# An MLP kernel whose first eight rows open with two token tiles, the third tile's input being loaded later

## The chip, the cores and the metric

The kernel runs on one core of one Trainium2 chip. The metric is the device time of one execution, in microseconds (us); the median of three runs before the change is 396.4 us (396.39, 396.40 and 397.09).

## What is computed

A channel MLP on 2048 tokens of 1024 channels, with a hidden width of 3584, all in bf16:

```python
def reference(x, w1, b1, w2, b2):
    y = _layernorm(x, axis=-1)            # over the 1024 channels, eps 1e-5
    h = _gelu(jnp.einsum("bsd,df->bsf", y, w1) + b1)     # tanh form
    return jnp.einsum("bsf,fd->bsd", h, w2) + b2
```

x is (1, 2048, 1024), w1 (1024, 3584), w2 (3584, 1024).

## The kernel before

Tokens are taken in 16 tiles of 128, four tiles to a block of 512 columns. The 1024 channels are eight groups of 128, called dt 0 to 7 here. The hidden units are 28 rows of 128. The first product of a block is made row by row: a row is eight matmuls, one for each dt, that accumulate in one PSUM bank (`pe_row`, L382). Gelu on ScalarE (`act_gelu`, L407) empties the bank to `hT_sb`, and the second product (`out_chunk`, L449) follows. Every engine has a program written out by hand in `_Prog` lists; for VectorE alone, the part after the first block's opening is merged from two lists (`crit` and `fill`) by estimated times.

The first eight rows of block 0 are made in another way, called the wave, because the input must first be loaded, transposed and normalised:

- Tiles 0, 1 and 2 are the raw tiles. TensorE transposes them as they were loaded (`pe_T`, L336), ScalarE copies the transposes from PSUM to `yT_sb` (L352), and the wave's matmuls (`pe_wave`, L397) run on values that aren't normalised. A cell is one row and one dt. Two columns of ones stand ahead of tile 0, so a cell on tiles 0 to 2 is 386 columns wide, a cell on tiles 0 and 1 is 258, and one on tile 2 alone is 128.
- Mean and variance of the raw tiles are taken on VectorE (`op_stats` L248, `op_aggr` L258), the power for the reciprocal deviation on GpSimd (L255). `ops_row_turn` (L480) turns them into rows, and `put_row_spread` (L486, ScalarE) spreads the rows over the partitions. `ops_fix` (L536 and L539) then corrects each wave row in PSUM, first by the mean and then by the deviation.
- Tile 3 is normalised before its matmul. VectorE does its statistics, its normalisation (L262) and a 32 by 32 block transpose (L490); ScalarE, VectorE and GpSimd move the blocks to their places (`put_moves_3` L507, `moves_3` L498 and L495). Its 64 cells of 128 columns come last in the wave, row by row, followed by each row's fix and gelu.
- From row 8 on, block 0 uses centred copies of the raw tiles, made by `ops_centre` (L529) on VectorE: four pieces, ctr0 to ctr3, of two dt each.

VectorE's order in the opening is one list:

```python
seq = st[0] + st[1] + st[2] + turn_m[:2] + st[3] + turn_m[2:] + nm[3] + moves_3() + turn_r + ctr[:2]
```

then the fixes of rows 0 and 1, ctr2 and ctr3, and the fixes of rows 2 to 7.

All loads but b1's are issued by SP on one queue, in the order of `SP_FIRST_LOADS`; x0 to x3 are 256 KB, and w0 to w8 are the nine pieces of w1 that the wave needs: w0 and w1 (128 KB each) hold dt 0 and dt 1 for rows 0 to 3, w2, w3 and w4 (256 KB) hold dt 2 and 3, 4 and 5, 6 and 7 for the same rows, and w5 to w8 hold the same for rows 4 to 7. The eight rows have the eight PSUM banks; from row 8 on, six banks are used in a ring, so row 8 waits for the gelu of row 0, and row 13 for that of row 7.

TensorE's order in the opening is: 25 matmuls on constants (L471), a small transpose for b1, the transposes of tiles 0, 1 and 2, four cells (rows 0 to 3 at dt 0) on tiles 0 and 1 and the same four on tile 2, then 28 cells of 386 columns (rows 0 to 3, dt 1 to 7), 32 of 386 columns (rows 4 to 7), and the 64 cells of tile 3.

Of the kernel before, what the change touches and what calls it, by code (L numbers as in the profile page):

```python
# [9 lines left out]
I32 = mybir.dt.int32  # L10

LN_EPS = 1e-5
P = 128
# [6 lines left out]
TAIL_PIECES = (448, 64)  # L20
RAW = (0, 1, 2)
N_WARM = 25
GROUPS_0 = (0, 4, 8)
GROUPS_2 = (0, 2, 8)
HALVES = (0, 4, 8)
PIECES = ((0, 1, (0, 1, 2, 3)), (1, 2, (0, 1, 2, 3)), (2, 4, (0, 1, 2, 3)), (4, 6, (0, 1, 2, 3)), (6, 8, (0, 1, 2, 3)),
          (0, 2, (4, 5, 6, 7)), (2, 4, (4, 5, 6, 7)), (4, 6, (4, 5, 6, 7)), (6, 8, (4, 5, 6, 7)))
CENTRE = (0, 2, 4, 6, 8)
DVE_MOVES = ((0, 0), (1, 1), (2, 2))
POOL_MOVES = ((3, 3), (0, 1), (1, 2), (2, 3))  # L30
W1_COLS = (512, 1024, 1024)
N_W2_CHUNKS = 4
SP_FIRST_LOADS = ("b1", "x0", "x1", "x2", "w0", "w1", "w2", "w3", "x3", "w4", "w5", "w6", "w7", "w8")
N_ONES = 2
PAD = 64

# [56 lines left out]
def bass_standalone__mixer_channel_mlp__prompt_kernel(  # L93
# [13 lines left out]
    DT = D // P  # L107
# [7 lines left out]
    R = R_WAVE  # L115
    assert R == NB1 + NB2 + 1 and R < FT
    assert NB1 + NB2 + 1 <= 8 and NB2 == 2
    assert all(c[-1] == DT for c in (GROUPS_0, GROUPS_2, HALVES))
    assert TPB == 4 and RAW == (0, 1, 2)

    w1_chunks = [(j0, j1, rows[0] * P, (rows[-1] + 1) * P) for j0, j1, rows in PIECES]
# [21 lines left out]
    with ExitStack() as es:  # L143
# [6 lines left out]
        yT_sb = sb("yT_sb", [P, 2, DT, PAD + TB], BF16)  # L150
# [26 lines left out]
        act = _Prog("s_act")  # L177
# [34 lines left out]
        def issue(item):  # L212
            if item == "b1":
                dma_q[0] = act
                dma(b1r_sb[:, :], b1.rearrange("(t p) -> t p", p=P), "b1", F * 2)
                dma_q[0] = sp
            elif item[0] == "x":
                load_x_tile(int(item[1:]))
            elif item[0] == "w" and int(item[1:]) < len(w1_chunks):
                load_w1(int(item[1:]))  # L220

        act.op(lambda e: e.preload_act_table(ACT.Gelu_apprx_tanh))
        for item in SP_FIRST_LOADS:
            issue(item)
# [8 lines left out]
        for b in range(2, NB):  # L233
# [4 lines left out]
                sig="ident")  # L238
# [53 lines left out]
        ybuf = lambda b: (b + 1) % 2  # L292
# [16 lines left out]
        def dve_put(o):  # L309
# [3 lines left out]
        bank_read = {}  # L313
        bank_of = {"t": ps_t[:, 0, :], "2_0": ps_2b[:, 0, :], "2_1": ps_2b[:, 1, :], "1_1": ps_1b[:, 1, :], "1_2": ps_1b[:, 2, :], "1_3": ps_1b[:, 3, :],
                   "1_4": ps_1b[:, 4, :]}
        ycol = lambda i: PAD + (i % TPB) * P
# [3 lines left out]
        def pe_T(i, groups, banks):  # L320
            blk = i // TPB
            src_ev = y_ev[i] if i in y_ev else [x_ev[i][0]] * DT
            evs = yT_ev.setdefault(i, [None] * DT)
            prev = None
            for k, (g0, g1) in enumerate(zip(groups[:-1], groups[1:])):
                bname = banks[k]
                for j in range(g0, g1):
                    waits = []
                    if bname != prev:
                        waits = ["ident"] + ([bank_read[bname]] if bname in bank_read else [])  # L330
                        off = 0
                    prev = bname
                    if j == g0 or src_ev[j] != src_ev[j - 1]:
                        waits.append(src_ev[j])
                    last = j == g1 - 1 and (k + 1 == len(banks) or banks[k + 1] != bname)
                    pe.op(lambda e, i=i, j=j, o=off, bap=bank_of[bname]: e.transpose(  # L336
                        out=bap[:, o:o + P], in_=x_sb[:, i, j * P:(j + 1) * P], identity=ident[:, :]),
                        waits=waits, sig=(f"tp{i}_{k}" if last else None))
                    evs[j] = f"te{i}_{k}"
                    off += P  # L340
            off = 0
            prev = None
            for k, (g0, g1) in enumerate(zip(groups[:-1], groups[1:])):
                bname = banks[k]
                if bname != prev:
                    off = 0
                prev = bname
                done = max(m for m in range(len(banks)) if banks[m] == bname)
                src = bank_of[bname][:, off:off + (g1 - g0) * P].bitcast(I32)
                src = src.rearrange("p (j s) -> p j s", j=g1 - g0)  # L350
                dst = yT_sb[:, 0 if i in RAW else ybuf(blk), g0:g1, ycol(i):ycol(i) + P].bitcast(I32)
                act.op(lambda e, dst=dst, src=src: e.copy(out=dst, in_=src), waits=[f"tp{i}_{done}"],  # L352
                       sig=f"te{i}_{k}")
                off += (g1 - g0) * P
                bank_read[bname] = f"te{i}_{k}"
            pe_t[0] += DT * 0.056

        unit_n = [0]
        bank_gelu = {}
# [4 lines left out]
        def new_unit():  # L364
            u = unit_n[0]
            unit_n[0] += 1
            bank = first_ring[u] if u < len(first_ring) else ring[(u - len(first_ring)) % len(ring)]
            waits = [bank_gelu[bank]] if bank in bank_gelu else []
            name = "t" if bank[0] == "t" else f"{bank[0]}_{bank[1]}"
            if not waits and name in bank_read:  # L370
                waits.append(bank_read[name])
            return bank, waits
# [16 lines left out]
        def pe_wave(r, dt, tiles, bank, waits, sig):  # L389
            raw = tiles[0] == 0  # L390
            base = raw_at if tiles[0] in RAW else 0
            y0 = ycol(tiles[0]) - (N_ONES if raw else 0)
            n0 = base + y0 - ycol(RAW[0]) if tiles[0] in RAW else 0
            n1 = n0 + ycol(tiles[-1]) + P - y0
            w = list(waits) + (["onecols"] if raw else []) + [yT_ev[t][dt] for t in tiles]
            w.append(f"w1c{w1_chunk_of(r, dt)}")
            pe.op(lambda e: e.matmul(  # L397
                unit_bank(bank)[:, n0:n1], lhsT=w1_sb[:, dt, r * P:(r + 1) * P], rhs=yT_sb[:, 0 if tiles[0] in RAW else ybuf(0), dt, y0:y0 + n1 - n0],
                start=(dt == 0 and tiles[0] in (0, 3)), stop=(dt == DT - 1), skip_group_check=True),
                waits=w, sig=sig)  # L400
            pe_t[0] += _mm_us(n1 - n0)
            if sig:
                est[sig] = pe_t[0]
# [80 lines left out]
        def put_row_spread(k, q0, q1):  # L484
            for q in range(q0, q1):
                act.op(lambda e, q=q: e.copy(out=row_b(k)[32 * q:32 * (q + 1)], in_=row_b(k)[0:32]),  # L486
                       waits=[f"row_q{k}"], sig=(f"row_{k}" if q == 3 else None))
# [27 lines left out]
        def put_b1():  # L515
            act.op(lambda e: e.copy(out=b1_sb[:, :], in_=bank_of["1_1"][:, 0:FT]), waits=["b1t"], sig="b1c")
            bank_read["1_1"] = "b1c"
# [5 lines left out]
        def ops_centre():  # L523
            res = []
            for k, (j0, j1) in enumerate(zip(CENTRE[:-1], CENTRE[1:])):
                xt, ct = [yT_sb[:, k, j0:j1, ycol(RAW[0]):ycol(RAW[0]) + len(RAW) * P].rearrange(
# [22 lines left out]

        pe_b1()  # L550
        put_b1()
        pe_T(0, GROUPS_0, ("t", "2_0"))
        pe_T(1, GROUPS_0, ("2_1", "1_4"))
        pe_T(2, GROUPS_2, ("t", "2_0"))
        put_row_spread(0, 1, 4)
        wave = [new_unit() for _ in range(R)]
        opened = set()

        def wave_cell(r, dt, tiles, sig=None):
            waits = [] if r in opened else wave[r][1]  # L560
            opened.add(r)
            pe_wave(r, dt, tiles, wave[r][0], waits, sig)

        first = [(r, dt) for r in PIECES[0][2] for dt in range(*PIECES[0][:2])]
        for tiles in (RAW[:2], RAW[2:]):
            for r, dt in first:
                wave_cell(r, dt, tiles)
        cells = [(r, dt) for j0, j1, rows in PIECES[1:] for r in rows if r < R for dt in range(j0, j1)]
        for n, (r, dt) in enumerate(cells):
            wave_cell(r, dt, RAW, f"raw_{r}" if dt == DT - 1 else None)  # L570
        cs_ev = {}
# [26 lines left out]
        for t in RAW:  # L598
            yT_ev[t] = [f"ctr{k}" for k, (j0, j1) in enumerate(zip(CENTRE[:-1], CENTRE[1:])) for _ in range(j0, j1)]

# [5 lines left out]
        for b in range(NB):  # L606
            if b + 1 < NB:
                tiles = list(range((b + 1) * TPB, (b + 2) * TPB))
# [9 lines left out]
            for st in range(TPB):  # L618
                for dh in range(DH):
                    c0, c1 = dh * NCH, (dh + 1) * NCH  # L620
                    ob = (b * TPB + st) % NOB
                    prev = store_last.get((ob, dh))
# [14 lines left out]
        while ci < len(crit) or fi < len(fill):  # L637
            take_crit = fi >= len(fill)
            if not take_crit and ci < len(crit):
                rel_f, _, blk_f = fill[fi]  # L640
                if crit[ci][0] <= max(t_dve, rel_f) + CRIT_SLACK and blk_f > crit[ci][2]:
                    take_crit = True
            if take_crit:
                rdy, o, _ = crit[ci]
                ci += 1
            else:
                rdy, o, _ = fill[fi]
# [46 lines left out]
```

## Time and profile before

| | us |
|---|---|
| median of three runs | 396.4 |
| the profiled execution, its own time | 396.67 |
| span of its profile | 395.4 |
| TensorE busy in the span | 390.9 |
| VectorE busy | 162.0 |
| ScalarE busy | 86.2 |
| GpSimd busy | 11.7 |

The profile is of one execution. Its span is 1.27 us shorter than that execution's time. A line of the timeline gives the start, the length, the engine, the line of the kernel, the operation, what it writes and reads, and how many instructions were merged; in brackets is the idle time of the engine before it, with what ended it. A matmul's listed length includes its way through the array, so neighbours overlap, and the pitch of a series is had from a window's length by the number of matmuls in it. The view of the DMA queues gives for each issue its size and the time from issue to landing.

### The profile page before, as it was taken

To read this page: it belongs to the slowest core of one execution; us is meant where nothing else is said; L and a number is where in the kernel's file an instruction comes from. 1 tells how busy PE (TensorE), PEld (TensorE's weight loads), DVE (VectorE), ACT (ScalarE), POOL (GpSimd) and SP (SyncE) were. 2 spreads that over 40 slices of the span, in tenths; PEclk is the share of its full clock that TensorE was granted. 3 is DMA by queue.
4 is the path that set the end of the run, shared out by engine and by line. 5 is a ranking of instruction groups with operands and counts; after the bars stand their busy time and mean duration, and the time that the engine had idled before them with its cause. 6 is when DMAs were issued, how large, how long until landed. Compare 5 with 4: busy or idle time off the path is not lost.

```text
span 395.4 us, 4518 instructions
## 1 busy us (share of the span) xinstructions
PE 390.9 (99%) x1904; PEld 184.9 (47%) x1938; DVE 162.0 (41%) x338; ACT 86.2 (22%) x139; POOL 11.7 (3%) x59
## 2 busy tenths in 40 slices
PE   9999999999999999999999999999999999999998
PEld 7744444444444444444444444444444444444444
DVE  5998889988999306987100000001100000001011
ACT  3655420000144332000023443100003334400000
POOL 3101000011001100000000000000000000000000
DMA  7999940000000000000000000000000000000000
GB/s 257 373 385 386 387 155 26 16 27 14 28 0 0 2 0 0 28 26 15 28 13 2 0 0 2 13 13 28 25 15 15 0 0 2 0 15 27 13 28 27
DMA packets 16078, 23.63 MB, mean 60 GB/s; under 512 B 1082, under 2 KB 8250, under 8 KB 16058
## 3 DMA queue, kind: packets, MB, share of 16 engines
q1 hardware_dynamic: 16016, 23.33, 16.7%
q8 instruction: 15, 0.25, 0.3%
q14 instruction: 5, 0.04, 0.0%
q10 hardware_dynamic: 42, 0.01, 0.0%
HBM read 19.14 MB, written 4.19 MB: 59 GB/s over the span
## 4 chain that ended last, share of the span: by engine, by line
PE 99%; issue 0%; DVE 0%
PE ps L449 49%; PE ps L382 38%; PE ps_t L382 7%; PE ps L397 3%; PE ps L471 1%; PE ps_t L397 0%; PE ps L336 0%; PE ps_t L336 0%; DVE o_sb L460 0%; PE ps L512 0%
## 5 line engine op out<-in xcount | busy, mean ns | idle before, releaser
L449 PE MATMUL ps<-w_sb,hT_sb 128*128 128x512 bf16 (+2 forms) x909 | 193.3, 373 | 0.8
L382 PE MATMUL ps<-yT_sb,w_sb 128*128 128x512 bf16 x678 | 152.4, 379 | 0.9
L449 PEld LDWEIGHTS ps<-w_sb,hT_sb 128*128 128x128 bf16 x924 | 88.6, 98 | 105.2
L407 ACT ACTIVATE hT_sb<-ps,b_sb 128x512 bf16<-128x512 f32 x94 | 64.0, 687 | 234.4 <-PE ps L382 217.2
L382 PEld LDWEIGHTS ps<-yT_sb,w_sb 128*128 128x128 bf16 x696 | 68.0, 98 | 81.9
L460 DVE TENSOR_TENSOR o_sb<-ps,b_sb 128x512 bf16<-128x512 f32 (+2 forms) x33 | 22.3, 675 | 198.7 <-PE ps L449 198.5
L304 DVE STREAM_TRANSPOSE yT_sb<-x_sb 32x256 bf16<-32x256 bf16 x192 | 83.7, 436 | 21.9 <-PE ps_t L382 18.8
L382 PE MATMUL ps_t<-yT_sb,w_sb 128*128 128x512 bf16 x135 | 31.9, 379 | 0.1
L248 DVE BATCH_NORM_STATS2 st_sb<-x_sb 128x6 f32<-128x512 bf16 x32 | 21.0, 672 | 4.7 <-DMA x_sb<-in_x_dram 4.6
L382 PEld LDWEIGHTS ps_t<-yT_sb,w_sb 128*128 128x128 bf16 x136 | 13.3, 98 | 16.1
L407 ACT ACTIVATE hT_sb<-ps_t,b_sb 128x512 bf16<-128x512 f32 x18 | 12.4, 687 | 17.5 <-PE ps_t L382 14.6
L397 PE MATMUL ps<-yT_sb,w_sb 128*128 128x128 bf16 (+2 forms) x116 | 13.1, 269 | 0.0
L397 PEld LDWEIGHTS ps<-yT_sb,w_sb 128*128 128x128 bf16 x116 | 8.9, 98 | 3.5
L255 POOL TENSOR_TENSOR rstd_sb<-mv_sb,nhalf 128x1 f32<-128x1 f32 x13 | 7.1, 548 | 113.6 <-DVE mv_sb L258 113.6
L423 DVE TENSOR_TENSOR ps<-ps,row_r 128x384 f32<-128x384 f32 x17 | 9.2, 561 | 2.7 <-PE ps L382 2.5
L262 DVE TENSOR_SCALAR x_sb<-x_sb,mv_sb,rstd_sb 128x1024 bf16<-128x1024 bf16 x13 | 7.0, 541 | 2.0 <-POOL rstd_sb L255 1.3
L536 DVE SCALAR_TENSOR_TENSOR ps<-row_r,ncs,ps 128x384 f32<-128x384 f32 x7 | 4.2, 614 | 0.6 <-PE ps L397 0.6
L486 ACT COPY row_r<-row_r 32x384 f32<-32x384 f32 x6 | 3.1, 510 | 4.3 <-DVE row_r L480 4.2
L539 DVE TENSOR_TENSOR ps<-ps,row_r 128x384 f32<-128x384 f32 x7 | 3.9, 563 | 0.2
L529 DVE TENSOR_TENSOR yT_sb<-yT_sb,row_r 128x768 bf16<-128x768 bf16 x4 | 3.6, 950 | 0.0
L471 PE MATMUL ps<-const-bfloat16-1.0 128*128 128x128 bf16 x25 | 2.8, 309 | 0.8 <-PEq L679 0.8
L258 DVE BATCH_NORM_AGGREGATE mv_sb<-st_sb 128x2 f32<-128x15 f32 x13 | 2.9, 222 | 0.4
(34 smaller groups left out, 32.9 us busy)
## 6 DMA issues: line engine op xcount, KB each, us to landing
w_sb<-in_w_dram SPq DMA_DIRECT2D x4, 1792.0 KB, 18.3
w_sb<-in_w_dram SPq DMA_DIRECT2D x2, 2048.0 KB, 16.4
out_dram<-o_sb SPq DMA_DIRECT2D x31, 128.0 KB, 1.7
x_sb<-in_x_dram SPq DMA_DIRECT2D x3, 1024.0 KB, 14.4
w_sb<-in_w_dram SPq DMA_DIRECT2D x7, 256.0 KB, 5.4
x_sb<-in_x_dram SPq DMA_DIRECT2D x4, 256.0 KB, 3.4
w_sb<-in_w_dram SPq DMA_DIRECT2D x1, 1024.0 KB, 10.1
w_sb<-in_w_dram SPq DMA_DIRECT2D x2, 128.0 KB, 3.7
```

Of the source, the lines that this page charges most:

```text
L248: return (lambda e, i=i, h=h, pw=pw: e.bn_stats(st_sb[i][:, 6 * h:6 * (h + 1)], x_sb[:, i, h * pw:(h + 1) * pw]), [x_ev[i][h if len(x_ev[i ...
L255: pool.op(lambda e, i=i, dst=dst, mv=mv: e.tensor_tensor(out=dst, in0=mv[:, 1:2], in1=nhalf[:, i:i + 1], op=ALU.pow), waits=[f"mv{i}", "nh ...
L262: return (lambda e, i=i, c0=c0, c1=c1: e.tensor_scalar(out=x_sb[:, i, c0:c1], in0=x_sb[:, i, c0:c1], scalar1=mv_sb[:, i, 0:1], scalar2=rst ...
L304: res.append((lambda e, src=src, dst=dst: e.transpose(out=dst, in_=src), waits, (f"tr{i}" if lastop else None), 0.47))
L382: pe.op(lambda e, b=b, r=r, dt=dt, bank=bank: e.matmul(unit_bank(bank)[:, 0:TB], lhsT=w1_sb[:, dt, r * P:(r + 1) * P], rhs=yT_sb[:, ybuf(b ...
L397: pe.op(lambda e: e.matmul(unit_bank(bank)[:, n0:n1], lhsT=w1_sb[:, dt, r * P:(r + 1) * P], rhs=yT_sb[:, 0 if tiles[0] in RAW else ybuf(0) ...
L407: act.op(lambda e, r=r, n0=n0, n1=n1, bank=bank: e.activation(out=hT_sb[:, r, n0:n1], in_=unit_bank(bank)[:, n0:n1], func=ACT.Gelu_apprx_tanh,
L423: crit.append((est[sig], (lambda e, reg=reg: e.tensor_tensor(out=reg, in0=reg, in1=row_b(1), op=ALU.mult), [sig, "row_1"], ready, 0.57), 0))
L449: pe.op(lambda e, sl=sl, ft=ft, c0=c0, c1=c1, bank=bank: e.matmul(ps_2[:, bank, 0:c1 - c0], lhsT=hT_sb[:, ft, sl * P:(sl + 1) * P], rhs=w2 ...
L460: crit.append((est[sig], (lambda e, ob=ob, c0=c0, c1=c1, bank=bank: e.tensor_tensor(out=o_sb[:, ob, c0:c1], in0=ps_2[:, bank, 0:c1 - c0], ...
L471: pe.op(lambda e: e.matmul(ps_1[:, 0, 0:P], lhsT=ones, rhs=ones, start=True, stop=True))
L536: return [(lambda e: e.scalar_tensor_tensor(out=reg, in0=row_b(0), scalar=ncs[:, c:c + 1], in1=reg, op0=ALU.mult, op1=ALU.add), [f"m1_0_{r ...
```

## The change

x2 is loaded four places later and x3 one place later: the order becomes x0, x1, w0, w1, w2, w3, x2, w4, x3, w5 and so on. Tiles 0 and 1 are copied in groups of two and six dt (before: four and four), and their copies alternate between the tiles. TensorE transposes tiles 0 and 1 only, then runs 24 cells of 258 columns (dt 0 to 5 of rows 0 to 3), then the transposes of tile 2, then 8 cells of 258 columns (dt 6 and 7), then 32 cells of 128 columns on tile 2 (dt 0 and 1 of the four rows first, as these are its first group), and after that rows 4 to 7 on all three tiles, now dt by dt where they were row by row within a piece. The mean's row spread on ScalarE stands behind tile 2's copies, as before. VectorE's list for the opening is the same; in the merged part behind it some statistics of block 1 stand one place earlier or later among the multiplications of rows 13 and on.

```diff
-GROUPS_0 = (0, 4, 8)
-GROUPS_2 = (0, 2, 8)
+GROUPS = (0, 2, 8)
...
+N_EARLY = 4
+N_PAIR = 5
...
-SP_FIRST_LOADS = ("b1", "x0", "x1", "x2", "w0", "w1", "w2", "w3", "x3", "w4", "w5", "w6", "w7", "w8")
+SP_FIRST_LOADS = ("b1", "x0", "x1", "w0", "w1", "w2", "w3", "x2", "w4", "x3", "w5", "w6", "w7", "w8")
...
+        def put_copy(i, groups, banks, k):
+            g0, g1 = groups[k:k + 2]
+            bname = banks[k]
+            assert banks.count(bname) == 1
+            src = bank_of[bname][:, 0:(g1 - g0) * P].bitcast(I32)
+            src = src.rearrange("p (j s) -> p j s", j=g1 - g0)
+            dst = yT_sb[:, 0, g0:g1, ycol(i):ycol(i) + P].bitcast(I32)
+            act.op(lambda e, dst=dst, src=src: e.copy(out=dst, in_=src), waits=[f"tp{i}_{k}"], sig=f"te{i}_{k}")
+            bank_read[bname] = f"te{i}_{k}"
...
-        pe_T(0, GROUPS_0, ("t", "2_0"))
-        pe_T(1, GROUPS_0, ("2_1", "1_4"))
-        pe_T(2, GROUPS_2, ("t", "2_0"))
-        put_row_spread(0, 1, 4)
+        T_BANKS = (("t", "2_0"), ("2_1", "1_4"), ("t", "2_0"))
+        for t in RAW[:2]:
+            pe_T(t, GROUPS, T_BANKS[t])
+        for k in range(2):
+            for t in RAW[:2]:
+                put_copy(t, GROUPS, T_BANKS[t], k)
...
-        first = [(r, dt) for r in PIECES[0][2] for dt in range(*PIECES[0][:2])]
-        for tiles in (RAW[:2], RAW[2:]):
-            for r, dt in first:
-                wave_cell(r, dt, tiles)
-        cells = [(r, dt) for j0, j1, rows in PIECES[1:] for r in rows if r < R for dt in range(j0, j1)]
+        cells_of = lambda a, b: [(r, dt) for j0, j1, rows in PIECES[a:b] for dt in range(j0, j1) for r in rows]
+        for r, dt in cells_of(0, N_EARLY):
+            wave_cell(r, dt, RAW[:2])
+        pe_T(2, GROUPS, T_BANKS[2])
+        for k in range(2):
+            put_copy(2, GROUPS, T_BANKS[2], k)
+        put_row_spread(0, 1, 4)
+        for r, dt in cells_of(N_EARLY, N_PAIR):
+            wave_cell(r, dt, RAW[:2])
+        for r, dt in sorted(cells_of(0, N_PAIR), key=lambda c: (c[1] >= GROUPS[1], c)):
+            wave_cell(r, dt, RAW[2:], f"raw_{r}" if dt == DT - 1 else None)
+        cells = cells_of(N_PAIR, len(PIECES))
```

`pe_T` itself loses its copies, which `put_copy` now issues.

More of the change, by code (lines that the diff above doesn't have):

```diff
@@ L117, in bass_standalone__mixer_channel_mlp__prompt_kernel @@
     assert NB1 + NB2 + 1 <= 8 and NB2 == 2
-    assert all(c[-1] == DT for c in (GROUPS_0, GROUPS_2, HALVES))
+    assert all(c[-1] == DT for c in (GROUPS, HALVES))
     assert TPB == 4 and RAW == (0, 1, 2)
@@ L340, in pe_T @@
                     off += P
[L341 to L355, printed above, removed]
-            pe_t[0] += DT * 0.056
+            pe_t[0] += DT * 0.056
+        def put_copy(i, groups, banks, k):
[7 more added lines that the diff above has]
+            bank_read[bname] = f"te{i}_{k}"
         unit_n = [0]
```

## The prediction

> **What bounds the kernel now.** First the page's first part and its chain of waits, for the whole span:
>
> ```profile
> PE 390.9 (99%) x1904; PEld 184.9 (47%) x1938; DVE 162.0 (41%) x338; ACT 86.2 (22%) x139; POOL 11.7 (3%) x59
> ...
> PE 99%; issue 0%; DVE 0%
> ```
>
> TensorE is the bound from end to end, so an edit of the opening can win only what TensorE loses there, and can lose what it is made to wait. So I read the chain's pieces in the opening (start, length, what):
>
> ```profile
> 0.83 2.82 PE ps L471 x25
> ...
> 4.32 1.28 PE ps L336 x12
> 5.60 0.10 issue
> 5.71 0.37 PE ps_t L336 x2
> 6.08 0.47 PE ps L336 x6
> 6.54 6.22 PE ps L397 x42
> ```
>
> The reader is to see that hardly a hole is left. The last transpose of tile 1 starts at 5.29 and those of tile 2 at 5.71, when x2 has landed (5.57); at a pitch of 0.107 us that is a pause of some 0.3 us. The second loss is speed: the 16 transposes from 3.71 start 0.107 us apart, and from 6.2 us on the same form starts 0.056 apart. The granted clock reads 1.00 throughout, so I take this from the spacing. What is left of the opening is full-speed work: windows over the wave give 4.57 us for 28 cells of 386 columns (0.163 each), 0.44 for 4 cells of 258 (0.110), and 3.57 for tile 3's 64 cells of 128 (0.056).
>
> Then the timeline, for the engines that walk close beside TensorE:
>
> ```profile
> 6.40 1.22 DVE L248 BATCH_NORM_STATS2 st_sb<-x_sb 128x6 f32<-128x512 bf16 x2
> ...
> 9.07 1.28 DVE L248 BATCH_NORM_STATS2 st_sb<-x_sb 128x6 f32<-128x512 bf16 x2 [0.61 <-DMA x_sb<-in_x_dram]
> ...
> 13.14 2.75 ACT L507 COPY yT_sb<-xq_sb 32x128 int32<-32x128 int32 x9 [0.16 <-DVE xq_sb L490]
> ...
> 16.84 3.29 PE L397 MATMUL ps<-yT_sb,w_sb 128*128 128x128 bf16 x56
> ...
> 17.49 1.15 DVE L536 SCALAR_TENSOR_TENSOR ps<-row_r,ncs,ps 128x384 f32<-128x384 f32 x2 [0.58 <-PE ps L397]
> ...
> 19.48 1.81 DVE L529 TENSOR_TENSOR yT_sb<-yT_sb,row_r 128x768 bf16<-128x768 bf16 x2
> ```
>
> VectorE takes tile 2's statistics at 6.40, straight behind tile 1's, and waits only for x3 (0.61 us). From 9.07 to 16.91 it runs without a hole, ScalarE's nine moves of tile 3 hang on it and end at 15.90, and TensorE starts tile 3's cells at 16.84: 0.94 us of air. VectorE waits 0.58 us for TensorE at 17.49, and is then full until 28 us. Behind that the air is thin: ctr3 is done at 21.30 and row 8's weight load for dt 6 stands at 21.50 (0.20); the gelu of row 7 signals at 28.76 and row 13, which takes its bank, loads weights at 28.84 (0.08). A weight load takes 0.098 us and stands 0.21 ahead of its matmul, which gives some 0.1 more.
>
> Last the queue. These are x2 (issued 1.69), w3 (3.59) and x3 (4.10), with the time to landing:
>
> ```profile
> x_sb<-in_x_dram SPq DMA_DIRECT2D x1, 256.0 KB, 3.9
> ...
> w_sb<-in_w_dram SPq DMA_DIRECT2D x1, 256.0 KB, 4.3
> ...
> x_sb<-in_x_dram SPq DMA_DIRECT2D x1, 256.0 KB, 4.9
> ```
>
> In order, the last parts land at 3.52 (x0), 4.15 (x1), 5.57 (x2), 5.94 (w0), 6.29 (w1), 6.98 (w2), 7.88 (w3), 9.05 (x3), 9.79 (w4). SP issues one about every 0.5 us, 3 to 5 us ahead of landing, so the bytes ahead decide, not the issue.
>
> **The change, part by part.**
>
> *The loads.* By bytes ahead, the new order lands w0 and w1 where x2 landed (w1 by 5.57; w0 midway from 4.15, 4.9), w2 at 6.29, w3 at 6.98, x2 (sixth 256 KB) where w3 landed, 7.88, w4 at 9.05, x3 at 9.79. But x2 and x3 took 1.42 and 1.17 us behind the piece before them, w3 only 0.90; x2 at 1.42 behind 6.98 would be 8.40. I take 8.1 for x2. Its upper bound is 9.05, where the eighth load landed before; its lower, w2's 6.98 plus w2's own step, 0.69, is 7.67. The loads behind x3 keep their bytes ahead, so their landings stay.
>
> *Transposes and copies.* Tiles 0 and 1 are transposed as before, the last starting at 5.29. ScalarE copies 128x128 in 0.27 us and 128x384 in 0.48 (rows of L352), with about 0.04 between. A transpose group signals 0.33 after its last start: tile 1's first group at 4.98, its copy done at 5.28; the big copies done at 5.80 and, after a signal at 5.62, at 6.33. Before, the first cells waited for tile 1's last copy, and it cost nothing as tile 2 was being transposed; now the first cells need only 5.28 and w0 (4.9), and start at about 5.4. The pause of 0.3 us is gone.
>
> *The first 24 cells.* 258 columns at half speed take 0.107 x 258/128 = 0.215 (an estimate; no row has this form so early). Four reach 6.28. Full speed from 6.2 us as before: dt 1 to 6.72 (w1 5.57), dt 2 and 3 to 7.60 (copies 6.33, w2 6.29), dt 4 and 5 to 8.47 (w3 6.98).
>
> *Tile 2.* Its transposes start at 8.47, with x2 at 8.1 no wait, and take 8 x 0.056 to 8.92. Then the cells of dt 6 and 7 need w4, 9.05: a wait of 0.15. 8 x 0.110 brings 9.98; ScalarE's copies of tile 2 (0.27 + 0.48 behind 8.9) lie beside them. 32 x 0.056 ends at 11.76. Before, this point was 11.62. So the gain of the early start, 0.3 us of pause at half speed (0.15) and eight transposes at full instead of half speed, is spent on running four wide cells at half speed, on the w4 wait, and on 28 splits at 0.110 + 0.056 - 0.163, 0.003 each, 0.08 together. TensorE on its own: +0.14. Bounds: without the w4 wait 0.0; with x2 at 9.05, +0.6.
>
> *Rows 4 to 7 dt by dt* cost nothing: the same cells, on weights landed (w5 at 10.52 against 11.76). Only raw_4 signals later (16.5), and ScalarE asks for it after 16.9. *The merge* moves a 0.68 us statistic ahead of row 13's multiplication; that bank is next wanted at row 19, five rows of 1.73 us later. Nothing.
>
> *What is late next.* Tile 2's statistics stand ahead of x3's in VectorE's list, so x2's landing now moves all behind it. Before, from 6.40 to the end of the first two turns took 2.07 us; with x2 at 8.1 they end at 10.2, after x3 (9.79), and x3's statistics start at 10.19, not 9.07: a shift of s = 1.12 us. Bounds of s: 0.74 (x3 alone decides) and 2.07 (x2 at 9.05). The tile 3 moves end at 15.90 + 1.12 = 17.02 against TensorE's 16.98: no more than 0.05. VectorE had 0.58 us of idle before the fixes; the rest, 0.54, is a late VectorE from there, with no hole until row 7's gelu. TensorE meets it at ctr3 and at row 13, whose air is 0.08 + 0.1. So TensorE's delay is s - 0.58 - 0.18 = **s - 0.76 = 0.36 us**, the 0.14 above lying within it. After row 13 the air is over 1 us (row 14's bank frees 29.34, wanted 30.78), and what TensorE has lost stays lost.
>
> *The sum.* 396.67 + 0.36 for the profiled execution. That stands 0.27 over the median, so the forecast for the median is 396.4 + 0.36, rounded **396.75 us**.
>
> **A rule against the change.** The half-speed row first: starts of 0.107 us from 0.83 to 6.19. The Trainium skill, page "TensorE: Matmul & The Clock Gate", section "What's actually happening", says that the clock is granted by a window of about 3.4 us that runs freely, and by how busy the array was in it. The trace agrees that a pause of 0.3 us at 5.4 did not put it off. By this rule the early cells get no sooner to full speed than the transposes did, which is what the sum has.
>
> **Rivals.** (1) *The gain stays.* If x2 lands by 7.74, x3 decides, s is 0.74 and VectorE's lateness is covered; w4 then tends to be early too, and TensorE runs from 11.6: 396.4. For it: the fastest of the engines' parts of x3 was there at 7.49, so the bytes allow it. Against: the last part decides, and both x2 and x3 trailed.
>
> (2) *Slower: x2 holds VectorE.* The place is tile 2's statistics, the price s - 0.76 with s = x2 - 6.98; over 0.8 us from x2 at 8.54 on. At the bound 9.05 it is +1.31, 397.7. For it: x2 lands amid the time (7 to 9 us) in which the eighth load trailed by 1.17. Against: 256 KB less lie ahead of it.
>
> (3) *The clock falls back.* Should the changed gap at 5.4 us begin the half-speed stretch (5.4 us, 0.83 to 6.2) anew, work until 10.8 is at half speed: 4.6/2 = +2.3, 398.7. Against: the pause in the trace of before did nothing of the kind. By the Trainium skill's window of 3.4 us it would be 1.7 (an estimate).
>
> (4) *Faster beyond measure.* The opening lost 0.15 by the pause and no more than 0.8/2 = 0.4 if full speed came at 5.4; both together are 0.55, and VectorE's chain would have to come along. Only the spread of runs, 0.7 us, could show it.
>
> **How the numbers follow.** A measurement of this kernel can tell about 0.2%, 0.8 us, from no change. Forecast (x2 from 7.75 to 8.54, 396.4 to 397.2): 0.47. Rival 1: 0.16. Rival 2: 0.27. Rival 3: 0.05. Rival 4: 0.05. Within 0.2% are the forecast and rival 1, 0.63; slower 0.32; faster 0.05. The range reaches to 397.7, rival 2's bound, and to 396.1, rival 1 less the spread seen below a median; about 0.15 stays outside.
>
> **What would show it.** In the profile after: no pause of TensorE at 5.4 to 5.7; an idle VectorE from 6.5 until x2 lands, about 1.6 us, under tile 2's statistics; x3's statistics at 10.2; the fixes at 18.0, no longer waiting for TensorE; small issue gaps of TensorE at row 8's dt 6 or at row 13; row 8 of block 0 at 20.5 to 20.8, where it stood at 20.36. Everything behind 31 us is the same, shifted. Wrong it would be if x2 lands after 8.54 or before 7.7, if w0 is not there at 5.4, or if TensorE's first cells keep the 0.215 pitch beyond 6.3 us.

## The result, and the profile after

The changed kernel takes 397.5 us (median of 17 runs, 396.75 to 398.86) against 396.52 us before (17 runs, 395.98 to 397.09): a ratio of 1.0025, with a 95% interval of 1.0016 to 1.0034. That is 0.98 us slower, where the forecast had 0.36. The median is inside the stated range because the range reached to the second rival's bound, 397.7; it lies 0.75 over the forecast's 396.75. The spread of the runs has doubled, from 1.1 to 2.1 us, and the fastest changed run, 396.75, lies within the runs of before.

The profiled execution took 398.02 us, with a span of 396.8, 1.4 more than before. The first part of its page and the shares of its chain of waits:

```profile
PE 391.3 (99%) x1932; PEld 186.3 (47%) x1966; DVE 161.4 (41%) x338; ACT 86.1 (22%) x139; POOL 11.7 (3%) x59
...
PE 97%; DMA 1%; issue 1%; SPq 0%; DVE 0%
```

TensorE is busy 0.4 us longer in a span 1.4 us longer, so 1.0 us is waiting. The chain now begins in the load queue. Its pieces in the opening (start, length, what):

```profile
2.64 5.05 DMA w_sb<-in_w_dram
7.69 0.14 issue
7.83 1.92 PE ps L393 x16
...
17.93 0.16 PE ps_t L393
18.09 0.12 issue
18.21 3.29 PE ps L393 x56
```

The first line is w2, issued at 2.64 and landed at 7.69; the forecast had 6.29. The timeline of the same kernel shows what stood still (start, length, engine, line, operation; in brackets the idle time before it and what ended it):

```profile
7.83 1.92 PE L393 MATMUL ps<-yT_sb,w_sb 128*128 128x258 bf16 x16 [0.90 <-DMA w_sb<-in_w_dram]
9.12 1.29 DVE L249 BATCH_NORM_STATS2 st_sb<-x_sb 128x6 f32<-128x512 bf16 x2 [2.68 <-DMA x_sb<-in_x_dram]
...
11.26 1.29 DVE L249 BATCH_NORM_STATS2 st_sb<-x_sb 128x6 f32<-128x512 bf16 x2
...
18.18 3.14 PEld L393 LDWEIGHTS ps<-yT_sb,w_sb 128*128 128x128 bf16 x56 [0.48 <-ACT yT_sb L503]
```

TensorE waits 0.90 us for w2. VectorE waits 2.68 us for x2, which landed at 9.10 (forecast 8.1), and takes x3's statistics at 11.26 where it took them at 9.07 before: s is 2.19 us. Tile 3's cells then wait for ScalarE's moves, which hang on VectorE. They start at 18.21 against 16.84, 1.37 us late, and the rest of the kernel is shifted by as much (row 8's second cell at 21.99 against 20.63).

Both late loads stand behind a dip in the load rate. Windows of the changed kernel (stretch, its length, granted clock, busy share of the load engines, GB/s):

```profile
4.00:5.00 1.00, 1.00 0.57 111
5.00:6.00 1.00, 1.00 0.80 216
6.00:7.00 1.00, 1.00 1.04 357
```

The kernel before moved 298 and 369 GB/s in the first two of these, at shares of 0.97 and 1.07. In the dip the engines are in part idle (a share of 0.57) and in part slow (111 GB/s at that share is less for each busy engine than 357 at 1.04).

The dip is not all of it. A load lands in 16 parts and counts as landed when the last part is there. The trace has each part's time: fifteen of w2's parts were there by 6.97 and the last at 7.69, fifteen of x2's by 8.40 and the last at 9.10. In the kernel before the last part trailed the fifteenth by 0.24 (w2) and 0.28 us (x2).

### The profile page after: what moved, and what is told of

Its sections match the earlier page's. It is cut to its first block, busy times and chain, and to the rows that moved or that the text cites. A ratio compares the mean times of both kernels' runs of the same rounds, so it can differ in the third digit from the quotient of the medians.

```text
span 396.8 us, 4574 instructions
## 1 busy us (share of the span) xinstructions
PE 391.3 (99%) x1932; PEld 186.3 (47%) x1966; DVE 161.4 (41%) x338; ACT 86.1 (22%) x139; POOL 11.7 (3%) x59
## 4 chain that ended last, share of the span: by engine, by line
PE 97%; DMA 1%; issue 1%; SPq 0%; DVE 0%
PE ps L445 49%; PE ps L378 38%; PE ps_t L378 7%; PE ps L393 3%; DMA w_sb<-in_w_dram 1%; PE ps_t L393 0%; SPq L190 0%; PE ps L337 0%; DVE o_sb L456 0%; PE ps_t L337 0%
## 5 line engine op out<-in xcount | busy, mean ns | idle before, releaser
L378 PEld LDWEIGHTS ps<-yT_sb,w_sb 128*128 128x128 bf16 x696 | 68.1, 98 | 81.9
L393 PE MATMUL ps<-yT_sb,w_sb 128*128 128x128 bf16 (+2 forms) x144 | 14.5, 252 | 1.0 <-DMA w_sb<-in_w_dram 0.9
L393 PEld LDWEIGHTS ps<-yT_sb,w_sb 128*128 128x128 bf16 x144 | 10.3, 99 | 3.9 <-issue 1.3
L393 PE MATMUL ps_t<-yT_sb,w_sb 128*128 128x386 bf16 (+1 forms) x16 | 3.2, 273 | 0.0
```

The lines of the kernel that those rows point to most:

```text
L378: pe.op(lambda e, b=b, r=r, dt=dt, bank=bank: e.matmul(unit_bank(bank)[:, 0:TB], lhsT=w1_sb[:, dt, r * P:(r + 1) * P], rhs=yT_sb[:, ybuf(b ...
L393: pe.op(lambda e: e.matmul(unit_bank(bank)[:, n0:n1], lhsT=w1_sb[:, dt, r * P:(r + 1) * P], rhs=yT_sb[:, 0 if tiles[0] in RAW else ybuf(0) ...
```

## The experiments

In what follows s is how much later than before VectorE starts x3's statistics. "TensorE's own" is how much later than before the last 386-column cell has run, which is before any wait for tile 3. Theory V says that VectorE, waiting for x2, sets the loss; theory T, that TensorE's own waits for loads do.

**The changed kernel once more**

> The changed kernel once more, for a second trace of its loads. In its first trace w2 landed at 7.69 us and x2 at 9.10, 1.4 and 1.0 us behind the forecast, after a dip of the load rate between 4.0 and 5.5 us (129, 100 and 129 GB/s in half microseconds, where before had 320 or more until 6.0). If the new order makes the dip, it is there again, w2 lands after 7.0 and row 8 starts 0.9 to 1.5 us behind its place before. If it was an accident of one execution, w2 lands at 6.3 to 6.6 and row 8 is 0.2 to 0.5 us late. Time 397.3 to 397.7 by both.

397.54 us (5 runs), 1.0032 (1.0019 to 1.0044). The traced run is the slowest of the five, 398.58. The dip is there again, shallower:

```profile
4.00:5.00 1.00, 1.00 0.81 235
5.00:6.00 1.00, 1.00 1.09 299
6.00:7.00 1.00, 1.00 0.93 298
```

w2 landed at 8.33, x2 at 9.65; s is 2.74, TensorE's own 1.72, and tile 3's cells start 1.93 late, more than the 0.9 to 1.5 us that were expected. TensorE's wait for w2:

```profile
5.04 1.15 PE L393 MATMUL ps<-yT_sb,w_sb 128*128 128x258 bf16 x8 [0.22 <-ACT yT_sb L351]
8.46 1.92 PE L393 MATMUL ps<-yT_sb,w_sb 128*128 128x258 bf16 x16 [2.27 <-DMA w_sb<-in_w_dram]
```

Here a single part did it: fifteen of w2's parts were there by 6.25, which is what the forecast had for the whole load, and the last came 2.08 us later, behind one packet that took 1.87 us (from 5.69). Of x2's parts fifteen were there by 8.19.

In all five traces of this order of loads (the two of the changed kernel and the three that follow next) w2 landed later than the forecast's 6.29, at 6.75 to 8.33, and x2 at 8.09 to 9.87. Fifteen of x2's parts were there by 8.02 to 8.40, and it is the last part that spreads.

**VectorE freed from x2**

```diff
-                                                          x_sb[:, i, h * pw:(h + 1) * pw]),
-                    [x_ev[i][h if len(x_ev[i]) == parts(i) else 0]],
+                                                          x_sb[:, 1 if i == 2 else i, h * pw:(h + 1) * pw]),
+                    [x_ev[1 if i == 2 else i][0]],
```

> The changed kernel, with tile 2's statistics taken from tile 1's data, so that VectorE doesn't wait for x2 (the output's tile 2 is normalised by another tile's figures). Theory V (VectorE late through x2, TensorE's delay is s - 0.76): s falls from 2.19 to what x3 sets (landing 10.55 in the first trace: 1.50), so the time falls by 0.4 to 0.7 us, to 396.9. Theory T (TensorE's own waits for w2 and x2 set its delay, 1.25 us at the end of row 7's wide cells in the first trace): no change, within 0.2 us of the changed kernel.

397.13 us (8 runs), 1.0018 (1.0008 to 1.0028): 0.4 less than the changed kernel, the lower end of what V expected, with intervals that overlap. The edit did its work, tile 2's statistics started at 6.43. But in the traced execution (398.35, its slowest) s did not fall (2.23), because x3 was late itself: w3 landed only at 9.26 and x3 at 11.28, and this line of its timeline shows the other chain:

```profile
9.31 1.05 PE L393 MATMUL ps<-yT_sb,w_sb 128*128 128x258 bf16 x8 [1.12 <-DMA w_sb<-in_w_dram]
```

Here TensorE's own is 1.70 and the whole loss is 1.70.

**TensorE freed from w2 and w3**

```diff
+            wd = dt % 2 if r < 4 and 2 <= dt < 6 else dt
-            w.append(f"w1c{w1_chunk_of(r, dt)}")
+            w.append(f"w1c{w1_chunk_of(r, wd)}")
...
-                unit_bank(bank)[:, n0:n1], lhsT=w1_sb[:, dt, r * P:(r + 1) * P],
+                unit_bank(bank)[:, n0:n1], lhsT=w1_sb[:, wd, r * P:(r + 1) * P],
```

> The changed kernel, with the cells of dt 2 to 5 of rows 0 to 3 taking the weights of dt 0 and 1, which have landed, so that TensorE doesn't wait for w2 and w3 (rows 0 to 3 get other weights there). Theory V: no change, within 0.2 us of the changed kernel, as VectorE still waits for x2. Theory T: the 0.9 us of waiting for w2 goes, but the transposes then wait for x2: the end of the wide cells comes 0.3 to 0.4 us sooner, and the time is 0.3 to 0.4 us less.

397.49 us (9 runs), 1.0029 (1.0019 to 1.0039): no change, as V expected. TensorE's own fell to 0.38, and what it had gained it gave back at tile 3's cells, in its weight loads:

```profile
16.90 0.10 PEld L394 LDWEIGHTS ps_t<-yT_sb,w_sb 128*128 128x128 bf16 x1
17.63 1.41 PEld L394 LDWEIGHTS ps<-yT_sb,w_sb 128*128 128x128 bf16 x25 [0.63 <-ACT yT_sb L504]
```

x2 landed at 8.55 there, s is 1.64, and the loss is 0.81.

**Both freed**

The two edits together.

> Both edits together: VectorE doesn't wait for x2, the cells of dt 2 to 5 don't wait for w2 and w3. Theory V alone: as with VectorE freed alone, 0.4 to 0.7 us less than the changed kernel. Theory T alone: as with the weights freed alone, 0.3 to 0.4 us less. If both chains are late by nearly the same, as the first trace has it (1.43 and 1.25 us), neither edit alone does much (0.0 to 0.2) and both together take 0.4 to 0.6 us off.

396.89 us (11 runs), 1.0011 (1.0002 to 1.0020): 0.6 off. s is 0.78, as x3 landed at 9.82, and TensorE's own is 0.24, which is the loss. By the medians alone theory V would do: 0.4 off with VectorE freed, nothing with TensorE freed, 0.6 with both, where two chains late by nearly the same should have given 0.0 to 0.2 for the first. It is the traces that show both chains: TensorE's own sets the loss with VectorE freed (1.70), VectorE sets it with TensorE freed (0.81). The loss is the larger of the two, and both are fed by late loads.

**The loads of before under the new cells**

```diff
-N_PAIR = 5
+N_PAIR = 4
-SP_FIRST_LOADS = ("b1", "x0", "x1", "w0", "w1", "w2", "w3", "x2", "w4", "x3", "w5", "w6", "w7", "w8")
+SP_FIRST_LOADS = ("b1", "x0", "x1", "x2", "w0", "w1", "w2", "w3", "x3", "w4", "w5", "w6", "w7", "w8")
```

> The changed kernel with the loads in the order of before (x2 third), and without the early wait for w4 (tile 2's cells of dt 0 to 5 stand directly behind its transposes, dt 6 and 7 run at full width). Theory V (the load order makes VectorE late): x3 lands near 9.1 and s is near 0; what is left is TensorE's own, cells that wait for w0 until 5.94 and for w3 until 7.88 and end 0.3 us later: 396.7 to 396.8. Rival (the order of the cells costs by itself): still 397.2 or more with VectorE on time. The rate of the loads has no dip below 230 GB/s before 6.5 us if the dip belongs to the new load order.

397.52 us (9 runs), 1.0032 (1.0022 to 1.0042). VectorE is on time (s is -0.03), the load rate has no dip (271 and 360 GB/s at shares of 0.98 and 1.03), and the time is as bad as that of the changed kernel, which is what the rival expected. The traced run, its fastest at 397.23, lost 0.53 us: the first cells waited for w0 until 5.90, later cells 0.22 us for w2 (one pitch of 0.334 in a series of 0.110), and tile 2's cells, now directly behind the transposes, 0.28 in two places for ScalarE's copies. That is TensorE's own 0.53, against 0.3 expected, and it left half of the median's loss open. So the same kernel ran again:

> The changed kernel with the loads of before once more, as its first trace was of its fastest run (397.23 against a median of 397.52, row 8 0.53 us late) and doesn't show what its median lost (1.1 us). VectorE is on time again (s within 0.2 of 0). If TensorE's waits for weights explain the median, row 8 is 0.8 to 1.2 us late with waits for w0, w2 or w3 of that sum; if the full speed of TensorE comes late in such runs, after the longer pause at 5.4, the spacing of 0.21 us for the 258 column cells lasts beyond 6.4 us.

398.00 us (7 runs: 397.37 to 398.99), 1.0035 (1.0021 to 1.0050). The traced run took 398.92. The same 24 cells of 258 columns, first in that run and then in the first one:

```profile
6.12 4.52 PE L393 MATMUL ps<-yT_sb,w_sb 128*128 128x258 bf16 x24 [0.52 <-ACT yT_sb L351]
```

```profile
5.90 3.02 PE L393 MATMUL ps<-yT_sb,w_sb 128*128 128x258 bf16 x24 [0.50 <-POOL stat_r L256]
```

The pause ahead of both lines is the wait for w0, which landed at 5.99 and 5.76; where the view names another releaser, that one had long been done. Nothing waits inside the longer line. Its starts are 0.215 us apart until 9.5 us and 0.110 from 9.7: TensorE ran at half speed for 3.4 us longer than in the trace of before (6.2), which costs 1.7 us, and tile 3's cells start 2.26 late with VectorE on time (s is -0.29). This is close to the prediction's third rival (there the half-speed stretch was to begin anew, here it went on), in a kernel that stops TensorE at 5.3 us for some 0.7 us. The first trace had a pause nearly as long, but full speed had come there at 5.0, ahead of it. That the pause is the cause is argued from these two traces; it was not varied. Three of its seven runs lie at 398.8 to 399.0 and the others at 397.4 to 398.0; only one of each kind was traced.

**Two issuing queues**

```diff
+                dma_q[0] = act if item in ("w0", "w1") else sp
                 load_w1(int(item[1:]))
+                dma_q[0] = sp
```

> The changed kernel with w0 and w1 issued by ScalarE's queue behind b1, so that SP issues w2, w3, x2, w4 and x3 about 0.94 us sooner. Theory S (the dip at 4.0 to 6.0 us comes from too few bytes issued: the 128 KB pieces are issued one in 0.47 us, 279 GB/s, less than the queue moves): the dip goes, w2 lands by 6.6, x2 by 8.2, s is 1.2 or less, 396.6 to 396.9. Theory P (the first packets of w1 are slow to come, whoever issues them, and only x packets beside them would fill the time): the dip stays below 230 GB/s, w2 lands after 7.0, 397.2 to 397.6.

397.12 us (10 runs), 1.0023 (1.0014 to 1.0032), between the two theories' times. The dip is gone:

```profile
4.00:5.00 1.00, 1.00 1.02 359
5.00:6.00 1.00, 1.00 1.03 304
```

x2 landed at 8.10, s is 1.19, both as theory S had it. But w1, now in the other queue beside three loads of SP's, landed at 6.90 (6.24 in the changed kernel's first trace; here fifteen of its parts were there by 6.01), and TensorE waited for it:

```profile
6.95 1.60 PE L395 MATMUL ps<-yT_sb,w_sb 128*128 128x258 bf16 x13 [0.85 <-DMA w_sb<-in_w_dram]
```

TensorE's own is 0.66 and the loss is 0.66.

**w0 and w1 as one load, twice**

```diff
-PIECES = ((0, 1, (0, 1, 2, 3)), (1, 2, (0, 1, 2, 3)), (2, 4, (0, 1, 2, 3)), ...
+PIECES = ((0, 2, (0, 1, 2, 3)), (2, 4, (0, 1, 2, 3)), ...
-N_EARLY = 4
-N_PAIR = 5
+N_EARLY = 3
+N_PAIR = 4
-SP_FIRST_LOADS = ("b1", "x0", "x1", "w0", "w1", "w2", "w3", "x2", "w4", "x3", "w5", "w6", "w7", "w8")
+SP_FIRST_LOADS = ("b1", "x0", "x1", "w0", "w1", "w2", "x2", "w3", "x3", "w4", "w5", "w6", "w7")
```

The bytes and their order are unchanged; the pieces of w1 are renumbered.

> The changed kernel with w0 and w1 as one load of 256 KB (dt 0 and 1 together), so that all behind it is issued 0.47 us sooner; order and bytes stay. Theory S: the dip is about half as deep, w2 and x2 land about 0.5 us sooner than in the changed kernel's traces (w2 at 7.69 and 8.33, x2 at 9.10 and 9.65), 397.0 to 397.3. Theory P: the dip and the landings are as in those traces, 397.4 to 397.6; the first cells may wait up to 0.4 us longer, as dt 0 comes with dt 1.

> The changed kernel with w0 and w1 as one load once more, for a second trace. Theory S (the dip comes from too few bytes issued ahead): between 4 and 5 us the load engines again have hardly a hole (all packets fill 0.95 or more of the time, against 0.60 and 0.80 in the changed kernel's two traces), x2 lands at 7.5 to 8.2, and the time is 396.8 to 397.1. Theory P (slow first packets of w1, a matter of luck): a dip as in the changed kernel is as likely as not, x2 at 8.5 to 9.5, and the five new times centre on 397.5.

396.98 us (11 runs), 1.0020 (1.0011 to 1.0029), then 396.81 us (11 runs), 1.0008 (0.9997 to 1.0019): 0.5 to 0.7 less than the changed kernel, for one load less to issue; the interval of the first still overlaps the changed kernel's. The stretch from 4 to 5 us in the first and in the second trace:

```profile
4.00:5.00 1.00, 1.00 0.98 316
```

```profile
4.00:5.00 1.00, 1.00 0.95 269
```

The engines' share is full in both. x2 landed at 7.69 and 7.81, s is 0.78 and 0.90, and tile 3's cells start 0.18 and 0.09 late. Fifteen of x2's parts were there by 7.53 and 7.71, and the last came 0.16 and 0.10 behind them. The dip went, as theory S had it, but x2 came 1.3 to 2.0 us sooner than in the changed kernel's two traces, where S had 0.5 for one issue less. With x2 sooner than the forecast's 8.1 and s below its 1.12, these traces lie between the forecast and its first rival; the medians stand 0.56 and 0.26 us over those of before, on either side of the forecast's 0.36.

**Versions between the two kernels**

`mid` puts w0 and w1 ahead of x2 and all else behind it; `merged_mid` does the same with merged pieces, x2 behind two of them; `before_merged` is the kernel before with w0 and w1 as one load.

```diff
-SP_FIRST_LOADS = ("b1", "x0", "x1", "w0", "w1", "w2", "w3", "x2", "w4", "x3", "w5", "w6", "w7", "w8")
+SP_FIRST_LOADS = ("b1", "x0", "x1", "w0", "w1", "x2", "w2", "w3", "x3", "w4", "w5", "w6", "w7", "w8")
-N_EARLY = 4
-N_PAIR = 5
+N_EARLY = 2
+N_PAIR = 2
```

> A version between the two: w0 and w1 ahead of x2, all else behind it as before; 8 cells on tiles 0 and 1, then tile 2's transposes, its 8 cells, and all further cells on three tiles. Theory V with TensorE's delay s - 0.76: x2 lands at 6.3 by bytes, x3 at 9.05 as before, so VectorE is on time (s below 0.5): 396.3 to 396.7. If w0 and w1 make the dip wherever they stand behind 512 KB of x, x2 lands at 7 to 8 and x3 at 9.6 to 9.9; s is 0.6 to 1.0: 396.5 to 396.9. TensorE's own can't go below the 396.4 of before by more than 0.1 or 0.2.

> The changed kernel with w0 and w1 as one load and x2 one 256 KB piece sooner: x0, x1, dt 0 and 1, dt 2 and 3, x2, dt 4 and 5, dt 6 and 7, x3; 16 cells on tiles 0 and 1, tile 2's transposes, its 16 cells, all else on three tiles. x2 lands near 7.0, x3 near 9.2, so s is 0.2 to 0.6 and VectorE's price s - 0.76 is below nothing; TensorE's own is near 0 (16 cells end at 7.6, after x2): 396.3 to 396.7, level with before. If the dip comes, x2 lands after 7.8 and it is 396.7 to 397.1.

> The kernel before with w0 and w1 as one load (8 cells on two tiles and 8 on tile 2 in place of 4 and 4); x2 stays third. x3 is issued 0.47 us sooner, but its bytes ahead are the same: it lands at 8.6 to 9.1. TensorE's work grows by 4 splits of 0.003 us. 396.2 to 396.5, no change that can be measured; if late pieces held before back at times, its slow runs (397.0) go away.

| | median us (runs) | ratio, interval | s | TensorE's own |
|---|---|---|---|---|
| mid | 397.06 (11) | 1.0018, 1.0009 to 1.0027 | 0.46 | 0.65 |
| merged_mid | 397.06 (11) | 1.0012, 1.0003 to 1.0021 | 0.44 | 0.50 |
| before_merged | 396.79 (11) | 1.0013, 1.0003 to 1.0023 | -0.16 | 0.47 |

All three were expected to be level with before, `mid` up to 0.5 and `merged_mid` up to 0.7 us slower if the dip came. `mid` and `before_merged` missed; `merged_mid` had the time of its dip (396.7 to 397.1) with a share of 0.93 between 4 and 5 us and x2 at 7.35, so its account missed too. VectorE was on time in all. The dip was in `mid` (157 GB/s from 4 to 5 us): x2 landed at 6.55 all the same, but w0 only at 5.49 and w2 at 8.21, and its cells waited 0.8 and 0.5 us for these two. In `merged_mid` the first load of weights landed at 5.97 and in `before_merged` x2 landed at 5.94, and TensorE waited from 5.1 or before until 6.1, on the first cells or on tile 2's transposes. Single parts again: fourteen of x2's parts in `before_merged` were there by 4.77. No version ran faster than before.

## Why the prediction came out as it did

- **What bounds the kernel, and what follows 31 us**: right. Beyond the opening nothing moved; the 1.4 us of the span is the 1.37 at tile 3's cells.
- **The rule of the sum**: right. The loss was to be s - 0.76, with TensorE's own within it if smaller. Over all fourteen traces, the larger of s - 0.8 and TensorE's own gives the start of tile 3's cells within 0.1 us (changed kernel: 1.39 and 1.08, measured 1.37; again: 1.94 and 1.72, 1.93; TensorE freed: 0.84 and 0.38, 0.82; two queues: 0.39 and 0.66, 0.66; before: none, 0).
- **Where the wait falls**: not as written. ctr3 and row 13 were to catch TensorE first; it was caught at tile 3's moves. Their air of 0.94 us is used up by an s over 0.8, and with the s of 1.6 to 2.7 that came, that wait is as long and stands earlier. The price is the same within 0.05, which is luck: the two places happen to have nearly the same air.
- **The landings**: this is the step that failed. The text had "SP issues one about every 0.5 us, 3 to 5 us ahead of landing, so the bytes ahead decide, not the issue". It put w2 at 6.29 and x2 at 8.1; the two traces have 7.69 and 8.33, 9.10 and 9.65. Bytes ahead did tell most of x2: fifteen of its sixteen parts were there by 8.40 and 8.19. Two things went wrong. The larger one is the size of a term: the prediction knew that the last part decides and took 8.1 instead of 7.88 for it, but the last part came 0.70 and 1.46 us behind the fifteenth, where x2 of before had 0.28. The other is the dip, for which the step left no room: with the same bytes in the same order and one load less to issue, fifteen of x2's parts were there by 7.53 and 7.71, the load engines' share was full, and 0.5 to 0.7 us came off. So the issue has some weight here, where the step gave it none. x2's measured landing is just beyond the upper bound that the prediction named (9.05) in the first trace and 0.6 us beyond it in the second.
- **TensorE's own**: forecast 0.14, measured 1.08 and 1.72. TensorE stood 0.90 and 2.27 us for w2, in the second trace at full speed from 3.7 on, which gave some of it back. In the first trace the early start (5.52 for 5.4), the 0.215 us pitch of the half-speed cells and the change to full speed near 6.3 came as described, and the pause at 5.3 to 5.7 shrank to 0.12 us; what it won was less than one wait for a late load.
- **Which case it was**: the second rival, x2 holding VectorE, which had 0.27, joined by a wait of TensorE's own nearly as long, which no rival had. The third rival, at 0.05, didn't show in the two traces of the changed kernel, but did in a kernel close to it. Whether the changed kernel's longest runs (398.4 and 398.9) are of that kind is open: the one at 398.58 that was traced was not, its loads were late.

What can't be settled here: why the last parts trail, and why the share dips. Trailing parts are in other orders too (0.89 us for w1 with two queues, 0.99 for w2 in `mid`), but not in the two traces with merged loads (0.10 to 0.18 for x2 and the load of dt 2 and 3); that is too few traces to say that the order makes them. Slow packets go with them in part (one of 1.57 and one of 1.87 us in the changed kernel's two traces, none over 0.75 before 9 us in the merged ones). For the dip, two queues kept the two small loads apart and lost it, which speaks for the issue; the number of issues and the number of separate loads were not varied apart otherwise. Nor were there enough traces to say how often the half speed lasts. And when full speed came differs between the traces (the last section), so TensorE's own is compared with a single trace of before, in which it came at 6.2.

## What to carry to other kernels

When a load is moved back in a queue to let another come early, follow every reader of the moved load, not just the engine that the edit is for: here tile 2's statistics stand ahead of tile 3's in VectorE's list, and waiting for x2 pushed these back too. Bytes ahead told when most parts of a load land; who waits for the load waits for its last part, and a bound needs room for that. One load of 256 KB did better than two of 128 KB in the changed kernel; in the other orders (`merged_mid` against `mid`, `before_merged` against before) no such gain can be seen. Here an opening at half speed gained little from being filled earlier, and an edit that makes it wait on loads takes over their scatter.

## What the runs showed of the hardware that was not expected

- With weights as the third and fourth load, 128 KB each, the load engines' busy share between 4 and 5 us was 0.57 to 0.81 (111 to 243 GB/s) in all six traces that issued them so on SP's queue behind x0 and x1; with the two as one load it was 0.93 to 0.98 in four traces, and 0.84 to 0.98 in the three where x2 stood ahead of the two.
- A load's last part can come long after the others: w2's sixteenth part at 8.33 us, the fifteenth at 6.25, in the changed kernel's second trace.
- How long TensorE runs at half speed differs between executions. By the spacing of its matmuls full speed came by 5.3 us in eight traces (in three of them by 3.7), between 6.2 and 6.7 in five (the kernel before at 6.2, the changed kernel's first trace at 6.3), and at 9.6 in one, the second trace of the loads of before, after a pause of 0.72 us from 5.3. That is 3.4 us later than in the kernel before. The Trainium skill, page "TensorE: Matmul & The Clock Gate", section "What's actually happening", has a freely running window of about 3.4 us that must be busy before the clock is granted, and these two traces agree with it. The granted clock in the windows view read 1.00 in the half-speed stretch too, so the spacing of the matmuls is what tells it.
